# A two-layer attention and MLP decode step: a ring of three places instead of four, and one more quarter of a key cache kept between the layers

## The chip, the cores and the metric

The kernel runs on one core of a Trainium2 chip. The metric is the device time of one execution in microseconds; lower is better. The engines are named as in the profile: PE multiplies matrices, DVE and POOL work on vectors, ACT evaluates activations and copies, SP issues the DMAs. SBUF is the on-chip memory of 128 partitions, PSUM the small memory that PE writes to.

## The reference

Two tokens (one for each of B = 2 batch rows) pass twice through the same attention block and the same gated MLP. All data are float32.

```python
# x (2, 1, 576); k_cache, v_cache (2, 32, 8192, 128); wq (576, 4096); wo (4096, 576)
# w_gate, w_up (576, 4608); w_down (4608, 576)
def A(x):                                       # attention, H = 32 heads, Dh = 128
    q = heads(x @ wq)
    p = softmax(q @ k_cache^T * Dh ** -0.5)
    return merge(p @ v_cache) @ wo
def B(x):                                       # GEGLU
    return (gelu(x @ w_gate) * (x @ w_up)) @ w_down
x = x + A(layernorm(x)); x = x + B(layernorm(x))   # layer 0
x = x + A(layernorm(x)); x = x + B(layernorm(x))   # layer 1, same caches, same weights
```

The two caches hold 268 MB each and do not fit in SBUF, so both layers read them from memory.

## The kernel before, in words

**Items.** A layer's attention is cut into 34 items. Items 0 to 29 are pairs of heads of one batch row, with 8 MB of keys and 8 MB of values each. Items 30 to 33 (`SINGLE`) are one head each, with keys and values in four quarters of 1024 KB (`PART`, 2048 numbers in each partition). K31 below means the keys of item 31, V33 the values of item 33. Layer 0 walks the items from 0 to 33, layer 1 from 33 to 0. What layer 0 used last can therefore stay for layer 1: K32 and K33 (`KEYS_HELD`), V31, V32 and V33 (`VALUES_HELD`), and one quarter of K31.

**The memory.** Loads go into one SBUF tile, `space`: five slots of four `PART`s, and behind them, at `RING`, a ring of `NPLACE` places of 1152 KB (`PLACE`). The slots hold keys and values. The ring carries what lies between the two walks: the eight groups of layer 0's `wo`, the first MLP's gate, up and down weights, layer 1's `wq`, and the first quarters of keys of layer 1. `arena` remembers who owns what.

**The order of the loads.** `plan_first`, `plan_mlp(0)`, `plan_second` and `plan_mlp(1)` write one list by hand. `pump()` issues its loads in that order on SP's queue (L165 caches, L296 and L298 `wo`, L238 and L227 `wq`, L248 and L258 gate and up, L271 and L275 down) as soon as their place has been handed over, and each `done(key)` frees a place and calls `pump()` again. SP is in order: a load that waits for its place to be read holds back every load behind it.

**Scores.** For a part of keys, `multiply` forms keys times query (L644 on DVE) and folds the two halves of the head dimension (L661 on POOL); `add_up` reduces them (L664 on DVE) and frees the part. For the first five items of layer 1 (33 to 29) the work is spread: of 16 rows in each partition DVE multiplies 12 and POOL 4 (L648), ACT sums 7 (L654) and DVE reduces 9; POOL's share uses a copy of the query (`qs`, L643 on ACT), made at an item's first part. Softmax, values (L762 on PE) and the division follow; `project` (L812) multiplies by `wo`. In layer 0 the products of K32 and K33 must not overwrite the keys, so they go into two buffers, which `products()` takes from places of the ring.

**The kept quarter.** In layer 0 ACT copies K31's quarter 3 to the PSUM tile `kept` (L636) before it is overwritten. In layer 1 quarters 0 to 2 of K31 are loaded again; when quarter 0 is summed, ACT copies `kept` into its place (L679), which then serves as quarter 3.

The MLP's matmuls are at L951 (gate and up) and L1004 (down), the normalization's transposes and means at L494 to L535, the query's matmul at L549. All line numbers are those of the kernel before.

Of the kernel before, what the change touches and what calls it, by code (L numbers as in the profile page):

```python
# [36 lines left out]
PART = JC * DH  # L37
SLOT = 4 * PART
NSLOT = 6
PLACE = DF // 2  # L40
NPLACE = 4
RING = 5 * SLOT
END = RING + NPLACE * PLACE
HELD = 5


# [17 lines left out]
SINGLE = range(PAIRS, N)  # L64
# [3 lines left out]
class Arena:  # L68
# [32 lines left out]
    def ring(self, key, n):  # L101

        at = self.take(key, RING + self.turn % NPLACE * PLACE, n)
        self.turn += at is not None
        return at

    def fit(self, key, n, lo=0):

        for at in [self.at, lo] + sorted(end for _, end in self.live.values()):
            if lo <= at and at + n <= END and self.take(key, at, n) is not None:  # L110
                self.at = at + n
# [11 lines left out]
def decode_layers(ctx, tc, x_in, kc, vc, wq, wo, wg, wu, wd, out):  # L123
    nc = tc.nc
# [7 lines left out]

    space = consts.tile([P, END], F32, name="space")

# [10 lines left out]
    arena = Arena()  # L145
    queue, ready, places = [], {}, {}

    def pump():
        while queue and queue[0]():
            queue.pop(0)  # L150

    def done(key):
        arena.free(key)
        pump()

    def part_at(at, n):
        return space[:, at:at + n]

    def part(at):
        return part_at(at, PART).rearrange("p (j d) -> p j d", d=DH)  # L160

    def load(at, n, src, lo, hi):

        t = part_at(at, (hi - lo) * PART).rearrange("p (j d) -> p j d", d=DH)
        nc.sync.dma_start(t, ITEMS[n].source(src)[:, lo * JC:hi * JC, :])  # L165

    def cache(key, src, n, slots=None, pieces=None):
# [14 lines left out]

        queue.append(make)

    def half(key, src, n, k, slot):

        def make():
            at = arena.slots(key, (slot,), 4, k)
            if at is None:
                return False  # L190
            load(at[0], n, src, k, k + 4)
            ready.setdefault(key, {}).update((k + i, part(a)) for i, a in enumerate(at))
            return True

        queue.append(make)
# [83 lines left out]
    def products():  # L279

        def make():
            at = [RING + k * PLACE for k in (2, 3)]
            if not all(arena.clear(a, PLACE) for a in at):
                return False
            ready["products"] = [part(arena.take(("products", k), at[k], PART)) for k in range(2)]
            return True

        queue.append(make)
# [28 lines left out]
    def groups(layer):  # L317
        return range(H // GH)[::1 - 2 * layer]

    def name(kind, layer, n):  # L320

        return kind, 1 if n in (KEYS_HELD if kind == "k" else VALUES_HELD) else layer, n

    def plan_first():
        def k(n, *at):
            cache(name("k", 0, n), kc, n, *at)

        def v(n, *at):
            cache(name("v", 0, n), vc, n, *at)

        for us in three:
            half_rows(("wq", 0, us[0]), wq, us, END - NU * H * DH // 2)
        last = PAIRS - 1
        k(0)
        for n in range(1, PAIRS):
            k(n)
            v(n - 1)
        k(SINGLE[0], (0,))
        half(("v", 0, last), vc, last, 0, 1)
        half(("v", 0, last), vc, last, 4, 5)  # L340
        k(SINGLE[1], (3,))
        v(SINGLE[0], (4,))

        k(SINGLE[2], (2,))
        products()
        k(SINGLE[3], (0,))
        v(SINGLE[1], (4,))
        v(SINGLE[2], (3,))
        for g in groups(0)[:2]:
            out_rows(0, g)  # L350

        v63 = ("v", 1, SINGLE[3])
        places[v63] = [SLOT + k * PART for k in range(4)]
        for k in range(4):
            if k == 2:
                for g in groups(0)[2:4]:
                    out_rows(0, g)
            one(v63, vc, SINGLE[3], k, (v63, k))
        for g in groups(0)[4:]:
            out_rows(0, g)  # L360

    def plan_second():

        for k in range(4):
            of_half(1, k)
        half_rows(("wq", 1, NU - 1), wq, single[-1], None)
        for k in range(4):
            of_half(0, k)
        last = PAIRS - 1
        k63, v63, k62, v62 = ("k", 1, SINGLE[3]), ("v", 1, SINGLE[3]), ("k", 1, SINGLE[2]), ("v", 1, SINGLE[2])  # L370

        for k in range(3):
            one(("k", 1, SINGLE[1]), kc, SINGLE[1], k, None)
        for k in range(4):
            one(("k", 1, SINGLE[0]), kc, SINGLE[0], k, (k63, k - 1) if k else None)

        one(("k", 1, last), kc, last, 0, (k63, 3))
        turns = iter(range(1, 5)), iter(range(4))
        for kind in "vvvvkkkk":
            if kind == "k":  # L380
                k = next(turns[0])
                one(("k", 1, last), kc, last, k, (k62, k - 1))
            else:
                k = next(turns[1])
                one(("v", 1, SINGLE[0]), vc, SINGLE[0], k, (v63, k))
        for k in range(5, 8):
            one(("k", 1, last), kc, last, k, (v62, k - 5))
        half(("k", 1, last - 1), kc, last - 1, 0, 5)
        half(("k", 1, last - 1), kc, last - 1, 4, 4)
        half(("v", 1, last), vc, last, 0, 0)  # L390
        half(("v", 1, last), vc, last, 4, 1)
        for n in range(last - 2, -1, -1):
            cache(("k", 1, n), kc, n)
            cache(("v", 1, n + 1), vc, n + 1)
        cache(("v", 1, 0), vc, 0, None, (4, 2, 1, 1))
        for g in groups(1):
            out_rows(1, g)
# [80 lines left out]
    kept = psum1.tile([P, JC, DH], F32, name="kept")  # L478
# [62 lines left out]
    def attention(layer):  # L541
# [30 lines left out]
        else:  # L572
            half_products(1)
            key = ("wq", 1, NU - 1)
# [55 lines left out]
        def multiply(n, k, m):  # L630

            if k == 0:
                S[n] = work.tile([P, SK * 2 // P], F32, name="S")
            u = t = keys(n, k, m)
            if n == SINGLE[1] and k == 3 and layer == 0:
                nc.scalar.copy(kept, t)  # L636
            if layer == 0 and n in KEYS_HELD:
                u = ready["products"][k % 2]
            every = m * JC
            rows = 12 if waited(n) else every  # L640
            q = qs[:, n % 2, :]
            if rows < JC and k == 0:
                nc.scalar.copy(q, qb[n])  # L643
            nc.vector.tensor_tensor(  # L644
                out=u[:, :rows, :], in0=t[:, :rows, :], in1=qb[n].unsqueeze(1).to_broadcast([P, rows, DH]), op=ALU.mult
            )
            if rows < JC:
                nc.gpsimd.tensor_tensor(  # L648
                    out=u[:, rows:, :], in0=t[:, rows:, :], in1=q.unsqueeze(1).to_broadcast([P, JC - rows, DH]),
                    op=ALU.mult,  # L650
                )
            r = own_rows(n, k, m)
            for j in range(r, every):
                nc.scalar.activation(  # L654
                    u[:, j, :], u[:, j, :], AF.Copy, accum_out=S[n][:, k * JC + j:k * JC + j + 1]
                )
            if at_once(n, k):
                prod[n, k] = u[:, :r, :]
                return
            half = prod[n, k] = u[:, :r, :DH // 2]  # L660
            nc.gpsimd.tensor_tensor(out=half, in0=half, in1=u[:, :r, DH // 2:], op=ALU.add)  # L661

        def add_up(n, k, m):
            nc.vector.tensor_reduce(  # L664
                out=S[n][:, k * JC:k * JC + own_rows(n, k, m)], in_=prod.pop((n, k)), axis=AX.X, op=ALU.add
            )
            if layer == 0 and n in KEYS_HELD:
                if n == N - 1 and k >= 2:
                    done(("products", k - 2))
                return  # L670
            key = name("k", layer, n)
            for k in range(k, k + m - 1):
                done((key, k))
            k += m > 1
            if layer == 1 and n == SINGLE[1]:

                if k == 0:
                    ready[key][3] = ready[key][0]
                    nc.scalar.copy(ready[key][3], kept)  # L679
                    return  # L680
                k = k % 3
            done((key, k))
            if k == ITEMS[n].parts - 1 or not any(c == key for c, _ in arena.live):
                ready.pop(key)
# [148 lines left out]
        for i, n in enumerate(seq):  # L833
            last = i == N - 1
            p = seq[i - 1] if i else None

            v = {N - 2: None, N - 1: N - 3}.get(i, i - 1) if layer == 0 else i - 1
            a = seq[i - 2] if i > 1 and completes(i - 2) and not (layer == 0 and last) else None
# [53 lines left out]
        n, p = seq[-1], seq[-2]  # L892
# [154 lines left out]
```

## Time and profile before

| | |
|---|---|
| median of 3 runs | 2686.73 us (2686.35 to 2687.53) |
| span of the profiled execution | 2685.0 us |
| bytes read | 1153.18 MB |
| busy: PE, DVE, ACT, POOL | 34%, 67%, 6%, 43% |
| loads' queue, share of 16 DMA engines | 99.8% |
| mean rate | 430 GB/s |

The span runs from the first to the last instruction of the profiled execution, which is 1.7 us shorter than the median. Times in the views are microseconds from the start of that span. Layer 0's attention ends at about 1290 us, its MLP at 1369, and layer 1's keys begin to load at 1384. In the timelines a row is: start, duration, engine, line, operation, output, inputs, count, and in brackets the idle time before with what ended it. In the table of windows a row is: window, then busy time and instruction count for PE, weight loads, DVE, ACT and POOL, the granted clock of PE, the DMA share and GB/s.

### The profile page before, as it was taken

What the parts mean: (1) busy time and instruction counts of PE and PEld (TensorE: products, weight loads), DVE (VectorE), ACT (ScalarE), POOL (GpSimd) and SP (SyncE); (2) the same over time, 40 slices, a digit from 0 to 9 for tenths busy, and PEclk for the clock granted to TensorE, in tenths of its full rate; (3) what the DMA queues carried; (4) which work ended last, traced back from release to release, by engine and by line L of the source; (5) the groups of instructions that cost most, each with busy time, mean ns of one, the idle gap of its engine ahead of it and who ended that gap; (6) DMA issues with size and microseconds to landing.
All of it is one profiled execution on the core that took longest, in us unless ns stands there. A gap on an engine that the chain in (4) does not pass through costs nothing. (4 is left out here: it accounts for less than half of the span.)

```text
span 2685.0 us, 17174 instructions
## 1 busy us (share of the span) xinstructions
PE 914.4 (34%) x7150; PEld 305.4 (11%) x7150; DVE 1806.0 (67%) x874; ACT 163.7 (6%) x786; POOL 1161.8 (43%) x261
## 2 busy tenths in 40 slices
PE   1323332332233233334663333233223323332356
PEld 0100010010001000111221101001000100010022
DVE  4876687677667766867037877667766776776640
ACT  0000000000000000000026000000000000000000
POOL 2543454354445444544028455445444543454420
PEclk7656666665666566566986665666566656656678
DMA  9999999999999999999999999999999999999998
GB/s 422 436 436 426 437 432 434 433 434 432 433 431 435 436 428 433 436 428 425 414 418 434 431 431 436 431 434 434 437 428 434 434 435 431 431 434 435 433 421 375
DMA packets 33950, 1154.30 MB, mean 430 GB/s; under 512 B 4152, under 2 KB 4176, under 8 KB 5968
## 3 DMA queue, kind: packets, MB, share of 16 engines
q1 hardware_dynamic: 33832, 1153.19, 99.8%
q8 instruction: 56, 0.92, 0.1%
q14 instruction: 22, 0.18, 0.0%
q10 hardware_dynamic: 40, 0.01, 0.0%
HBM read 1153.18 MB, written 0.00 MB: 429 GB/s over the span
## 5 line engine op out<-in xcount | busy, mean ns | idle before, releaser
L661 POOL TENSOR_TENSOR space<-space 128x3072 f32<-128x3072 f32 (+3 forms) x221 | 1128.6, 5107 | 1263.3 <-DVE space L644 1202.5
L644 DVE TENSOR_TENSOR space<-space,bank 128x6144 f32<-128x6144 f32 (+3 forms) x223 | 1112.7, 4991 | 560.2 <-DMA space<-in_A_k_cache_dram 496.8
L762 PE MATMUL acc<-space,prz 128*8 128x512 f32 x4096 | 594.6, 744 | 199.4 <-DMA space<-in_A_v_cache_dram 195.5
L664 DVE TENSOR_REDUCE S<-space 128x48 f32<-128x3072 f32 (+3 forms) x223 | 569.3, 2553 | 89.9 <-POOL space L661 89.6
L592 PE MATMUL bank<-qsb,pick 4*64 4x128 f32 (+1 forms) x256 | 46.3, 436 | 863.1 <-DVE space L644 853.1
L762 PEld LDWEIGHTS acc<-space,prz 128*8 128x8 f32 x4096 | 119.1, 104 | 616.3 <-issue 410.6
L784 PE MATMUL bank<-of,osb 128*32 128x2 f32 x512 | 40.9, 202 | 324.4 <-DVE osb L777 324.4
L713 ACT ACTIVATE nbs<-bank 128x2 f32<-128x2 f32 (+1 forms) x68 | 11.6, 171 | 1848.2 <-PE bank L698 1801.8
L592 PEld LDWEIGHTS bank<-qsb,pick 4*64 4x64 f32 (+1 forms) x256 | 20.7, 202 | 882.5 <-DVE space L644 863.2
L517 POOL TENSOR_TENSOR rstd<-ve,mhalf 128x1 f32<-128x1 f32 x4 | 2.2, 550 | 168.8 <-DVE ve L515 168.8
L690 PE MATMUL bank<-ident,m 128*1 128x128 f32 x68 | 19.5, 286 | 160.7 <-DVE m L688 160.5
L784 PEld LDWEIGHTS bank<-of,osb 128*32 128x32 f32 x512 | 35.9, 154 | 331.7 <-DVE osb L777 330.5
L978 DVE STREAM_TRANSPOSE o<-o 128x288 f32<-128x288 f32 x4 | 2.8, 691 | 94.5 <-ACT o L976 94.5
L729 PE MATMUL bank<-sums,unit 128*128 128x2 f32 x120 | 35.2, 363 | 87.0 <-ACT prz L721 87.0
L776 DVE TENSOR_TENSOR acc<-acc,diag 128x512 f32<-128x512 f32 x64 | 43.5, 680 | 22.0 <-PE acc L762 22.0
L721 ACT ACTIVATE prz<-S,nbs 64x128 f32<-64x128 f32 (+1 forms) x128 | 50.7, 396 | 17.3 <-POOL prz L711 14.4
L803 ACT ACTIVATE oT<-bank,rinv 32x8 f32<-32x8 f32 x110 | 28.5, 259 | 381.5 <-PE bank L784 380.8
L654 ACT ACTIVATE space<-space 128x128 f32<-128x128 f32 x164 | 48.3, 296 | 23.6 <-DVE space L644 21.7
L698 PE MATMUL bank<-m,unit 1*128 1x2 f32 (+1 forms) x136 | 39.0, 354 | 25.3 <-DVE m L696 25.3
L777 DVE TENSOR_REDUCE osb<-acc 128x128 f32<-128x512 f32 x64 | 44.3, 691 | 2.2
L521 DVE TENSOR_TENSOR x<-bank,x 128x144 f32<-128x144 f32 x4 | 1.2, 308 | 64.1 <-PE bank L1004 40.4
L729 PEld LDWEIGHTS bank<-sums,unit 128*128 128x128 f32 x120 | 30.1, 311 | 92.2 <-ACT prz L721 92.2
(73 smaller groups left out, 427.6 us busy)
## 6 DMA issues: line engine op xcount, KB each, us to landing
space<-in_A_v_cache_dram SPq DMA_DIRECT2D x8, 4096.0 KB
space<-in_A_k_cache_dram SPq DMA_DIRECT2D x6, 4096.0 KB
space<-in_A_wo_dram SPq DMA_DIRECT2D x15, 1152.0 KB
space<-in_A_k_cache_dram SPq DMA_DIRECT2D x15, 1024.0 KB
space<-in_B_w_down_dram SPq DMA_DIRECT2D x9, 1152.0 KB
space<-in_B_w_gate_dram SPq DMA_DIRECT2D x3, 3456.0 KB
space<-in_A_v_cache_dram SPq DMA_DIRECT2D x10, 1024.0 KB
space<-in_A_wq_dram SPq DMA_DIRECT2D x3, 3072.0 KB
```

Of the source, the lines that this page charges most:

```text
L592: nc.tensor.matmul(qb[n][to, :], pick[32 * c:32 * c + 4, r:r + 1].to_broadcast([4, P // it.heads]), qsb[32 * c:32 * c + 4, (h % 4) * DH:(h ...
L644: nc.vector.tensor_tensor(out=u[:, :rows, :], in0=t[:, :rows, :], in1=qb[n].unsqueeze(1).to_broadcast([P, rows, DH]), op=ALU.mult)
L654: nc.scalar.activation(u[:, j, :], u[:, j, :], AF.Copy, accum_out=S[n][:, k * JC + j:k * JC + j + 1])
L661: nc.gpsimd.tensor_tensor(out=half, in0=half, in1=u[:, :r, DH // 2:], op=ALU.add)
L664: nc.vector.tensor_reduce(out=S[n][:, k * JC:k * JC + own_rows(n, k, m)], in_=prod.pop((n, k)), axis=AX.X, op=ALU.add)
L698: nc.tensor.matmul(mT[n][:, :heads], ones[0:1, :], m1[:, :heads], start=True, stop=True)
L721: nc.scalar.activation(pr[at, lo:].rearrange("p (g e) -> p g e", e=4)[:, 0:it.rows // 2:2, :], s[at, :it.rows].rearrange("p (g r) -> p g r ...
L729: nc.tensor.matmul(tot[n][:, :ITEMS[n].heads], ones, rs.pop(n), start=True, stop=True)
L762: nc.tensor.matmul(accumulator(n)[32 * c:32 * c + 8, :], pr[:, at:at + 8], t[g // 4][:, g % 4 * 4:g % 4 * 4 + 4, :].rearrange("p j d -> p ...
L776: nc.vector.tensor_tensor(out=q, in0=q, in1=diag.unsqueeze(2).to_broadcast([P, 4, DH]), op=ALU.mult)
L777: nc.vector.tensor_reduce(out=t, in_=q.rearrange("p r d -> p d r"), axis=AX.X, op=ALU.add)
L784: nc.tensor.matmul(po[lo:lo + 32, i, :], t[:, i::GH], of, start=True, stop=True)
```

## The change

The ring has three places. The fourth place becomes `KEPT`, in which K31's quarter 3 is loaded in layer 0 and stays for layer 1; `SCRATCH`, the last part of slot 3, takes its products in layer 0. The PSUM tile `kept` now holds quarter 2 of K31: ACT copies it out in layer 0 one quarter earlier, and in layer 1 back into the place of quarter 0, where it serves as quarter 2. Layer 1 loads only quarters 0 and 1 of K31. The two buffers of `products()` move to places 1 and 2. In layer 0 the second half of V29 and the whole of K31 are each loaded as three parts and one part instead of four.

```diff
 PLACE = DF // 2
-NPLACE = 4
+NPLACE = 3
 RING = 5 * SLOT
-END = RING + NPLACE * PLACE
+KEPT = RING + NPLACE * PLACE
+END = KEPT + PART
+SCRATCH = 3 * SLOT + 3 * PART
...
+    def some(key, src, n, k, at):
+        def make():
+            if not all(arena.clear(a, PART) for a in at):
+                return False
+            for i, a in enumerate(at):
+                arena.take((key, k + i), a, PART)
+            load(at[0], n, src, k, k + len(at))
+            ready.setdefault(key, {}).update((k + i, part(a)) for i, a in enumerate(at))
+            return True
+        queue.append(make)
...
-            at = [RING + k * PLACE for k in (2, 3)]
+            at = [RING + k * PLACE for k in (1, 2)]          # products()
...
         half(("v", 0, last), vc, last, 0, 1)
-        half(("v", 0, last), vc, last, 4, 5)
-        k(SINGLE[1], (3,))
+        some(("v", 0, last), vc, last, 4, [5 * SLOT + k * PART for k in range(3)])
+        some(("v", 0, last), vc, last, 7, [SCRATCH])
+        k61 = name("k", 0, SINGLE[1])
+        some(k61, kc, SINGLE[1], 0, [3 * SLOT + k * PART for k in range(3)])
+        some(k61, kc, SINGLE[1], 3, [KEPT])
...
-        for k in range(3):
+        for k in range(2):
             one(("k", 1, SINGLE[1]), kc, SINGLE[1], k, None)
...
-            if n == SINGLE[1] and k == 3 and layer == 0:     # multiply()
-                nc.scalar.copy(kept, t)
+            if n == SINGLE[1] and layer == 0:
+                if k == 2:
+                    nc.scalar.copy(kept, t)
+                elif k == 3:
+                    u = part(arena.take(("scratch", 0), SCRATCH, PART))
...
+            if layer == 0 and n == SINGLE[1] and k == 3:     # add_up()
+                ready.pop(key)
+                ready["k", 1, n] = {3: part(KEPT)}
+                done(("scratch", 0))
+                return
...
                 if k == 0:
-                    ready[key][3] = ready[key][0]
-                    nc.scalar.copy(ready[key][3], kept)
-                    return
-                k = k % 3
+                    ready[key][2] = ready[key][0]
+                    nc.scalar.copy(ready[key][2], kept)
+                else:
+                    done({1: (key, 1), 2: (key, 0), 3: (("k", 0, n), 3)}[k])
+                if k == 3:
+                    ready.pop(key)
+                return
             done((key, k))
```

## The prediction

> **What bounds the kernel now.** I read the page first: busy time by engine, then the slices, then the DMA queues.
>
> ```profile
> span 2685.0 us, 17174 instructions
> PE 914.4 (34%) x7150; PEld 305.4 (11%) x7150; DVE 1806.0 (67%) x874; ACT 163.7 (6%) x786; POOL 1161.8 (43%) x261
> DMA  9999999999999999999999999999999999999998
> q1 hardware_dynamic: 33832, 1153.19, 99.8%
> HBM read 1153.18 MB, written 0.00 MB: 429 GB/s over the span
> ```
>
> No compute engine is above 67%, while the one load queue keeps the 16 DMA engines occupied for 99.8% of the span and no slice of 67 us falls below nine tenths except the last. So the time is bytes over rate, plus whatever time the queue runs dry. The profiled span is 2685.0 us; the three runs have a median of 2686.73 us, 1.7 us more. I work out differences against the profiled execution and add them to the median.
>
> Because the DMA is never visibly idle, the whole question is where the change could make it idle. That depends on how early each load is issued before the load ahead of it has landed. I read that lead from three views: the timeline of SP (when a load is issued), the waits of PE (a matmul that begins when a weight lands dates that landing), and the DMA view of one window for the rate there.
>
> **The load that goes.** The change removes one load of a quarter of K31, 1024 KB or 1.0486 MB. Rate at that place, from the DMA view of 1390 to 1437 us:
>
> ```profile
> DMA packets 2663, 20.02 MB, mean 426 GB/s; under 512 B 298, under 2 KB 298, under 8 KB 298
> space<-in_A_k_cache_dram SPq DMA_DIRECT2D x12, 1024.0 KB
> space<-in_A_v_cache_dram SPq DMA_DIRECT2D x4, 1024.0 KB
> ```
>
> 1.0486 MB / 426 GB/s = 2.46 us. That is the ceiling of the gain: 0.09% of the span. Two other loads of 4096 KB (V29's second half, K31 in layer 0) become 3072 + 1024 KB each, the same bytes in two more instructions. The Trainium skill, DMA: Bandwidth & Descriptors, section "Anatomy of one DMA", gives a fixed cost of about 2.0 us for each DMA beside its bytes; charged to every queued load it would take 4.0 us for the two splits and give back 2.0 with the removed one, so that the whole sum below would be 3.2 us and the time 2689.9 us. The rows above speak against charging it to a queued load: loads nearly all of 1024 KB run at 426 GB/s, so consecutive ones cost about their bytes and I take 0 for the splits.
>
> **What an idle queue costs to restart.** The only place in the trace where the queue starts from nothing is the beginning:
>
> ```profile
> 0.74 6.96 SPq L227 DMA_DIRECT2D space<-in_A_wq_dram  x3
> 0.00:1.00 1.00, 0.00 (x0) 0.00 (x0) 0.17 (x3) 0.00 (x0) 0.41 (x5) 1.00 0.00 0
> 1.00:2.00 1.00, 0.00 (x0) 0.00 (x0) 0.62 (x7) 0.00 (x0) 0.29 (x1) 1.00 0.95 246
> 2.00:3.00 1.00, 0.00 (x0) 0.00 (x0) 0.91 (x7) 0.00 (x0) 0.00 (x0) 1.00 0.42 147
> 3.00:4.00 1.00, 0.00 (x0) 0.00 (x0) 0.89 (x4) 0.00 (x0) 0.00 (x0) 1.00 0.92 393
> 4.00:5.00 1.00, 0.00 (x0) 0.00 (x0) 0.78 (x3) 0.00 (x0) 0.00 (x0) 1.00 1.04 444
> 2682.00 0.64 SPq L1019 DMA_DIRECT2D out_dram<-x  x1
> ```
>
> The last column is GB/s. By 5.00 us 246 + 147 + 393 + 444 = 1230 KB have come, worth 2.9 us at 430 GB/s; the data effectively began at 2.1 us, 1.4 us behind the issue at 0.74. The other end: the small store issued at 2682.00 has to be complete before the span ends at 2685.0, 3.0 us from issue to completion. So a load that is issued into an empty queue effectively starts 1.4 to 3.0 us after its issue. I take 2.7, near the upper end, because what releases work is the completion of the last of 16 engines, as in the store's row.
>
> **The ring with three places.** Here a place is loaded as soon as the matmuls of the load before it in that place are done.
>
> ```profile
> 1299.48 1.16 PE L951 MATMUL acc<-space,xt 128*8 128x288 f32 x16 [0.35 <-DMA space<-in_B_w_gate_dram]
> 1302.25 1.16 PE L951 MATMUL acc<-space,xt 128*8 128x288 f32 x16 [1.20 <-DMA space<-in_B_w_gate_dram]
> ```
>
> A place takes 2.77 us to land, and PE needs 1.16 us for it, after which SP issues. With four places three loads are queued behind a landing; with three, two: 2 x 2.77 - 1.2 = 4.3 us of lead, against a restart of 1.4 to 3.0. So the steady ring costs nothing; the cover left is 1.3 us. Three starts of the ring are tighter.
>
> ```profile
> 1233.48 0.86 SPq L296 DMA_DIRECT2D space<-in_A_wo_dram  x2
> 1234.39 0.90 SPq L165 DMA_DIRECT2D space<-in_A_v_cache_dram  x2
> SPq L296 <- DVE S L664: 23.1, 1, 23.1
> 1258.46 2.95 SPq L296 DMA_DIRECT2D space<-in_A_wo_dram  x2
> 1272.04 1.17 PE L812 MATMUL bank<-space,oT 128*4 128x144 f32 x32 [1.30 <-DMA space<-in_A_wo_dram]
> 1296.75 1.11 SPq L258 DMA_DIRECT2D space<-in_B_w_gate_dram  x2
> 1372.97 0.33 SPq L227 DMA_DIRECT2D space<-in_A_wq_dram  x1
> 1375.51 1.04 PE L549 MATMUL acc<-space,xt 128*4 128x512 f32 x8 [1.03 <-DMA space<-in_A_wq_dram]
> ```
>
> First, wo. The two product buffers of K32 and K33 move to places 1 and 2, so the second group of wo, which is now issued at 1233.9, waits with the third for DVE's last sums (1258.46, the wait of 23.1 us). Behind it on SP stand the first two quarters of V33. What lands at 1272.04 is the third wo group; taking off its 1152 KB (2.8 us), two quarters of V33 (4.9) and the second group (2.8), the first group lands at about 1261.5, 3.1 us after the new issue at 1258.46. That just covers the restart, with nothing to spare, so I take 0.2 us, 0 to 0.5. Second, the first MLP: its fourth gate piece now waits for the first piece's matmuls, which in this trace release the issue at 1296.75, and the third piece lands at 1299.48: lead 2.7 us, cost 0 to 0.3, taken 0.1. Third, layer 1's query weights: the fourth piece of the first half waits for the first piece's matmuls, behind the normalization (issue at 1372.97), and the third lands at 1375.51: lead 2.5 us, cost 0 to 0.5, taken 0.2. Sum 0.5 us (0 to 1.3). With these the order of the bytes is unchanged.
>
> **The copy from PSUM.** This is the part that decides, by my reading. In layer 1 item 31's four quarters are multiplied in order on DVE. The quarter in PSUM comes back by a copy on ACT (L679). Before it is the last quarter; after, the third. The timelines of ACT and DVE:
>
> ```profile
> 1421.45 1.84 ACT L679 COPY space<-kept 128x2048 f32<-128x2048 f32 x1
> 1427.00 0.30 ACT L654 ACTIVATE space<-space 128x128 f32<-128x128 f32 x1
> 1427.29 0.25 ACT L643 COPY qs<-bank 128x128 f32<-128x128 f32 x1
> 1419.60 1.73 DVE L644 TENSOR_TENSOR space<-space,bank 128x1536 f32<-128x1536 f32 x1
> 1423.32 1.75 DVE L644 TENSOR_TENSOR space<-space,bank 128x1536 f32<-128x1536 f32 x1 [0.28 <-ACT space L679]
> 1424.99 0.75 DVE L664 TENSOR_REDUCE S<-space 128x9 f32<-128x576 f32 x1
> 1427.58 1.75 DVE L644 TENSOR_TENSOR space<-space,bank 128x1536 f32<-128x1536 f32 x1 [1.83 <-ACT qs L643]
> ```
>
> The copy stands on ACT's in-order queue behind the second quarter's sums and a softmax, so it does not end sooner. DVE multiplies the third quarter at 1419.60 while the copy is still to come, and only the fourth waits for it, at 1423.32. After, the third waits until 1423.32. Then the fourth follows the third's 1.75 us and one reduction of 0.75, at about 1425.8, ending at 1427.5; ACT's seven sums of it, 0.30 us each, end at 1429.6; the query copy of item 30 (L643, 0.25), queued behind them, ends at 1429.85, and item 30's first multiply starts at 1429.9 instead of 1427.58: 2.3 us later. The quarter already in SBUF cannot help, as its multiply stands behind the third's on DVE.
>
> Who waits for it: the load of K28's first half, into the places of K31 and K30's first quarter. SP issues it when item 30's first quarter is summed.
>
> ```profile
> 1432.83 0.33 SPq L165 DMA_DIRECT2D space<-in_A_k_cache_dram  x1
> 1442.17 0.33 SPq L165 DMA_DIRECT2D space<-in_A_k_cache_dram  x1
> 1390.38 1.04 PE L549 MATMUL acc<-space,xt 128*4 128x512 f32 x8 [1.04 <-DMA space<-in_A_wq_dram]
> 1466.84 0.33 SPq L165 DMA_DIRECT2D space<-in_A_k_cache_dram  x1
> ```
>
> The last query weights land at 1390.38. Behind them come 19 loads of 1024 KB (15 of K, 4 of V), 19 x 2.46 = 46.7 us, so the queue is empty at 1437.1: K28's issue at 1432.83 has 4.3 us of lead, and no time is lost. After, 18 loads are left and the queue is empty at 1434.6, but the issue comes at 1432.83 + 2.3 = 1435.1, and data flow at 1435.1 + 2.7 = 1437.8 (1436.5 to 1438.1 over the restart's range). Against 1437.1 before: +0.7 us (-0.6 to +1.0). The 2.46 us are not lost to another transfer; they become 3.2 us of an empty queue.
>
> K28's second half (1442.17 + 2.3 = 1444.5) is issued 3.1 us before the first half's 4.19 MB end at 1437.8 + 9.8 = 1447.6, just covered. K27 (1466.84 + 2.3) has V29's 8.39 MB ahead of it, which end after 1437.8 + 39.4 = 1477, and keeps 8 us. From there all loads move as a block to the end.
>
> The ACT copy in layer 0 also moves one quarter ahead. DVE waits there 3.96 us for the load of K32, more than the copy's 1.84 us, so I take nothing:
>
> ```profile
> 1229.61 2.29 DVE L644 TENSOR_TENSOR space<-space,bank 128x2048 f32<-128x2048 f32 x1 [3.96 <-issue]
> ```
>
> The sum: +0.7 at K28, +0.5 at the ring's starts, +1.2 us. On the median that is 2687.9 us. Its own bounds: -0.6 + 0 to +1.0 + 1.3, that is 2686.1 to 2689.0.
>
> **The rivals.** (1) The plain gain. If the copy's move doesn't delay item 30, K28 is issued at 1432.83 with 1.8 us of lead before 1434.6, against a restart of 1.4 to 3.0: 0 to 1.2 us lost, 1.3 to 2.5 us gained, 2684.2 to 2685.4. For it: ACT is idle for long in the span (6% busy), and a scheduler might place the copy ahead. Against it: in the built program the copy has the same place in ACT's queue. (2) Slower: the ring. If a load in mid-stream needs more than 4.3 us from issue to landing beyond its own transfer, each of the 44 loads of the ring (8 of wo, 27 of the MLP, 9 of the query weights) loses the rest: at 4.6 us, 0.3 x 44 = 13 us, 2700 us; 0.13 us each is enough to be slower. For it: in the ring DMA moves less than elsewhere already,
>
> ```profile
> 1300.00:1310.00 10.00, 5.76 (x68) 1.83 (x60) 0.00 (x0) 0.00 (x0) 0.00 (x0) 1.00 1.00 398
> ```
>
> 398 GB/s. Against it: the busy share in the same row is 1.00, so the low rate is not a wait. (3) That no load goes away: the built program issues one load of a quarter less in layer 1, so I give it nothing.
>
> **The numbers.** One measurement of this kernel can tell about 0.2% from no change, 5.4 us, so faster means below 2681.4 and slower above 2692.1. The likeliest case (spent at K28) gets 0.65, the plain gain 0.20, the ring 0.13, and 0.02 is left for a gain beyond the removed bytes, for which I see no mechanism. All of the first two cases is within 0.2%: faster 0.02, same 0.85, slower 0.13. The range takes in the plain gain's end, 2684.2, and reaches upward from 2689.0 to the edge of the ring's case, 2692.0; left out are the ring and the unexplained gain, 0.15.
>
> **What would show it.** Right: in the timeline of SP after, K28's first half is issued about 2.3 us later than before, the copy is followed by the third quarter's multiply, and the DMA's rate falls in the window of 1434 to 1438; the waits keep SP's long wait for DVE at wo. Wrong: K28's issue no later than before (then the plain gain), or shares of DMA below 1.0 all through 1262 to 1390 us (then the ring). A change of more than 2.5 us downward would refute the bytes' price, and one of more than 2.4 us upward the restart's.

## The result, and the profile after

The changed kernel takes 2695.8 us (median of 5 runs, 2693.33 to 2699.6), the kernel before 2686.73 us (2686.35 to 2687.53): slower by a factor of 1.0035, 95% interval 1.0023 to 1.0048. I had forecast 2687.9 us and a range up to 2692.0. The profiled execution of the changed kernel spans 2694.0 us, 9.0 more than before, so its trace shows the whole loss. The five runs also spread over 6.3 us where five of before spread over 1.2.

The page of the changed kernel, busy time, slices and the load queue:

```profile
span 2694.0 us, 17166 instructions
PE 917.7 (34%) x7150; PEld 305.2 (11%) x7150; DVE 1805.8 (67%) x874; ACT 164.0 (6%) x786; POOL 1161.9 (43%) x261
DMA  9999999999999999999999999999999999999998
GB/s 421 435 435 434 430 431 434 430 435 432 433 432 434 435 434 431 429 429 414 395 391 416 438 429 435 431 434 434 433 433 434 431 433 435 429 433 433 433 423 376
```

The DMA's busy digits are the same as before, 9 in every slice but the last. Only the line below them has changed: 414, 395, 391 and 416 GB/s in slices 19 to 22, that is 1212 to 1482 us. Before, it read 425, 414, 418 and 434 at that place:

```profile
GB/s 422 436 436 426 437 432 434 433 434 432 433 431 435 436 428 433 436 428 425 414 418 434 431 431 436 431 434 434 437 428 434 434 435 431 431 434 435 433 421 375
```

The loss lies between the two walks, where the ring is.

The same stretch as one window, before and after (the last three columns are PE's granted clock, DMA busy share, GB/s):

```profile
1260.00:1400.00 140.00, 87.56 (x1105) 34.98 (x1095) 24.89 (x52) 10.76 (x59) 8.83 (x8) 0.94 1.01 416
```

```profile
1260.00:1400.00 140.00, 91.69 (x1105) 34.62 (x1097) 17.10 (x46) 5.23 (x22) 4.17 (x6) 0.91 1.00 394
```

The rate falls by 5.3%, from 416 to 394 GB/s, while the busy share only falls from 1.01 to 1.00 (by the DMA records from 1.006 to 0.991, which is 2.1 us of the 140). At the old rate the same bytes would have come 140 x (1 - 394/416) = 7.4 us earlier. DVE's busy time, 24.89 and 17.10 us, says the same: layer 1's scores begin later.

Where in the ring it accrues is read from matmuls that begin when a load lands. Before, then after: the third wo group, the last up piece of the first MLP, its last down piece (only after, where the row before was at 1367.25 us), and the last query weights.

```profile
1272.04 1.17 PE L812 MATMUL bank<-space,oT 128*4 128x144 f32 x32 [1.30 <-DMA space<-in_A_wo_dram]
1342.70 1.16 PE L951 MATMUL acc<-space,xt 128*8 128x288 f32 x16 [1.23 <-DMA space<-in_B_w_up_dram]
1367.25 1.16 PE L1004 MATMUL bank<-space,hT 128*4 128x144 f32 x32 [0.62 <-DMA space<-in_B_w_down_dram]
1390.38 1.04 PE L549 MATMUL acc<-space,xt 128*4 128x512 f32 x8 [1.04 <-DMA space<-in_A_wq_dram]
```

```profile
1273.04 1.16 PE L841 MATMUL bank<-space,oT 128*4 128x144 f32 x32 [2.15 <-DMA space<-in_A_wo_dram]
1346.11 1.16 PE L980 MATMUL acc<-space,xt 128*8 128x288 f32 x16 [1.42 <-DMA space<-in_B_w_up_dram]
1372.36 1.16 PE L1033 MATMUL bank<-space,hT 128*4 128x144 f32 x32 [0.67 <-DMA space<-in_B_w_down_dram]
1398.45 1.04 PE L567 MATMUL acc<-space,xt 128*4 128x512 f32 x8 [0.96 <-DMA space<-in_A_wq_dram]
```

The delay is 1.0 us at wo, 3.4 at the end of gate and up, 5.1 after down, 8.1 after the query weights (by the DMA records 0.6 us of it is there before the ring, at the first wo group). It grows along the whole ring, not at one place.

The part that I had called decisive is there too. DVE, ACT and SP of the changed kernel at item 31 and at K28's first and second half:

```profile
1429.53 1.84 ACT L705 COPY space<-kept 128x2048 f32<-128x2048 f32 x1
1431.40 1.75 DVE L665 TENSOR_TENSOR space<-space,bank 128x1536 f32<-128x1536 f32 x1 [3.65 <-ACT space L705]
1433.80 1.75 DVE L665 TENSOR_TENSOR space<-space,bank 128x1536 f32<-128x1536 f32 x1
1437.92 1.75 DVE L665 TENSOR_TENSOR space<-space,bank 128x1536 f32<-128x1536 f32 x1 [1.70 <-ACT qs L664]
1443.16 0.33 SPq L167 DMA_DIRECT2D space<-in_A_k_cache_dram  x1
1452.30 0.33 SPq L167 DMA_DIRECT2D space<-in_A_k_cache_dram  x1
```

The third quarter waits for the copy, 3.65 us. From that multiply to item 30's first are 6.5 us (forecast 1429.9 - 1423.3 = 6.6), and K28's issue follows 5.2 us behind that (forecast 5.2).

### The profile page after: what moved, and what is told of

It reads as the page before. It is cut to its first block, busy times and chain, and to the rows that moved or that the text cites. A ratio compares the mean times of both kernels' runs of the same rounds, so it can differ in the third digit from the quotient of the medians.

```text
span 2694.0 us, 17166 instructions
## 1 busy us (share of the span) xinstructions
PE 917.7 (34%) x7150; PEld 305.2 (11%) x7150; DVE 1805.8 (67%) x874; ACT 164.0 (6%) x786; POOL 1161.9 (43%) x261
## 5 line engine op out<-in xcount | busy, mean ns | idle before, releaser
L742 ACT ACTIVATE nbs<-bank 128x2 f32<-128x2 f32 (+1 forms) x68 | 11.6, 171 | 1847.1 <-PE bank L727 1800.7
```

## The experiments

**The ring alone, the order alone, the products alone, and two places.** Four kernels, measured on one chip together with the kernel before.

```diff
 # ring3_only: the kernel before with
-NPLACE = 4
-END = RING + NPLACE * PLACE
+NPLACE = 3
+END = RING + 4 * PLACE
-            at = [RING + k * PLACE for k in (2, 3)]
+            at = [RING + k * PLACE for k in (1, 2)]
 # and item 30's first quarter at RING + 3 * PLACE
```

> The kernel before with a ring of three places and the product buffers in places 1 and 2; the fourth place is left empty, except that it takes item 30's first quarter of keys in layer 1. All three quarters of K31 are loaded again and the last comes from PSUM, as before: no load is removed and the copy is not moved. Theory R (the ring loses the time: in the changed kernel the loads' landings fall 7.9 us behind those of before between the first wo group and the first quarter of K31): about 2694 us, 6 to 10 us above before, with a wider spread of runs than before. Theory C (the copy's move at the start of layer 1 and the product buffers at wo make most of the loss): 2687 to 2689 us.

Measured: 2695.71 us (2693.97 to 2699.32), ratio 1.0033 (1.0021 to 1.0046). Three places (with the products' move that they need), with every load still there and the copy in its old position, cost 9.0 us: as much as the whole change, with a similar spread of runs, 5.4 us. Its window:

```profile
1260.00:1400.00 140.00, 87.62 (x1105) 34.45 (x1097) 17.24 (x46) 5.23 (x22) 3.61 (x4) 0.95 0.99 393
```

```diff
 # copy_last: the changed kernel with, in units(),
+            if layer == 1 and n == SINGLE[1]:
+                return [(k, 1) for k in (0, 1, 3, 2)]
 # and K31 is handed over after quarter 2
```

> The changed kernel, but in layer 1 item 31's quarters are multiplied in the order 0, 1, 3, 2, so that the quarter copied back from PSUM is the last again. Theory R: the ring's 8 us stay; K28's first half is issued about 2.3 us earlier relative to item 31's start, and 1 to 2.3 us are won against the changed kernel: 2693.5 to 2695 us. Theory C: 2687 us or less. If the copy's place costs nothing: 2695.8 us as the changed kernel.

Measured: 2695.38 us (2692.12 to 2696.32), ratio 1.0030 (1.0019 to 1.0041). The ring's loss stays. Against the changed kernel the median is 0.4 us lower, less than the spread of either, so this pair doesn't size the copy; copy_third below measures it in the kernel before.

```diff
 # products12: the kernel before with
-            at = [RING + k * PLACE for k in (2, 3)]
+            at = [RING + k * PLACE for k in (1, 2)]
```

> The kernel before with four places, and one edit: the product buffers lie in places 1 and 2 instead of 2 and 3, so that the second wo group and two quarters of V33 wait for DVE's last sums as in the changed kernel. My prediction gave this step 0.2 us (0 to 0.5): 2686.9 us. If the lead that the DMA engines lose there is paid back later in the ring: 2688 to 2690 us.

Measured: 2687.58 us (2687.18 to 2689.86), ratio 1.0004 (0.9995 to 1.0013). The medians are 0.9 us apart and the interval holds 1, so the step is small; the interval's upper end, 3.5 us, still leaves most of the 9 us to the place count.

```diff
 # ring2_only: the kernel before with NPLACE = 2; products, K31's third
 # and item 30's first quarter in the two places beside the ring
```

> The kernel before with a ring of two places; products, K31's third and item 30's first quarter have places of their own beside the ring, so nothing else waits longer. With two places one load of 2.77 us is queued behind a landing, less 1.2 us of matmuls: 1.6 us of lead. A restart of 2.7 us, as predicted, makes each of some 44 loads lose 1.1 / 2 to 1.1 us: 25 to 50 us. A restart of 4 to 5 us on the slowest engine (theory R's reading of why three places lose) makes it 2.4 to 3.4 us each or half of that: 55 to 150 us.

Measured: 2729.63 us (2724.14 to 2730.37), ratio 1.0160 (1.0145 to 1.0176): 43 us, 1.0 us for each of 44 loads. That lies in the range of my restart, not in that of the longer one.

**Halved places.** In the same memory, twice as many loads of half the size. They were meant to lengthen the lead.

```diff
 # half_places: copy_last with
+HALF_PLACE = PLACE // 2
-        at = self.take(key, RING + self.turn % NPLACE * PLACE, n)
-        self.turn += at is not None
+        at = self.take(key, RING + self.turn % (2 * NPLACE) * HALF_PLACE, n)
+        self.turn += (1 if n <= HALF_PLACE else 2) if at is not None else 0
 # and each ring load and its matmuls in two halves; half_before: the same in the kernel before
```

> The changed kernel with item 31's quarters multiplied in the order 0, 1, 3, 2, and with the ring cut into six places of 576 KB in the same memory: every weight load of the ring is halved, and each half is freed after its own matmuls. If a ring of three places loses because 4.3 us queued behind a landing is too little for the slowest engine's restart (2.5 to 5.4 us from issue to data in the two-place run), the lead of 5 x 1.39 - 0.7 = 6.2 us brings nearly all of the ring's 8 to 9 us back: 2685.5 to 2688 us. If it loses because of the number of separate loads or places that are handed over, twice as many make it worse: 2700 us or more.

> The kernel before with its four places cut into eight of 576 KB in the same way: what halving the loads costs by itself, where the lead was already enough (7.1 us, now 9 us). 2686.5 to 2688 us if rows of half the length move at the same rate; 2690 us or more if shorter rows or more issues on SP cost a few per cent of the 125 us in which the ring is read.

Measured: half_places 2698.36 us (2697.39 to 2699.09), ratio 1.0043 (1.0030 to 1.0055); half_before 2692.35 us (2691.47 to 2693.98), ratio 1.0021 (1.0012 to 1.0030). Halving costs 5.7 us in the kernel with four places. The window from 1310 to 1345 us, of half_before and then of before, shows a full busy share at a lower rate:

```profile
1310.00:1345.00 35.00, 21.75 (x221) 5.47 (x214) 1.87 (x7) 0.97 (x3) 0.00 (x0) 0.95 1.02 408
```

```profile
1310.00:1345.00 35.00, 20.50 (x216) 6.79 (x216) 2.34 (x8) 1.47 (x4) 0.00 (x0) 0.95 1.01 422
```

But the lead did not become longer. SP's waits in the same window (total us, times, longest) are, in half_before and then in before:

```profile
SPq L254 <- DMA space<-in_B_w_up_dram: 3.5, 15, 0.8
SPq L254 <- DMA space<-in_B_w_gate_dram: 2.8, 14, 0.2
SPq L267 <- PE acc L989: 0.2, 1, 0.2
```

```profile
SPq L248 <- PE acc L951: 7.0, 5, 1.6
SPq L248 <- DMA space<-in_B_w_gate_dram: 4.0, 5, 1.0
```

Before, SP waits mostly for the matmuls that free a place. In half_before it waits for earlier loads to land. These programs count the landings of their loads on eight semaphores, and no trace of this case has more than eight loads issued and not landed; from 1290 to 1345 us 62 of half_before's 73 issues come within 0.1 us of the landing of the load eight before. A piece of gate or up is two loads, so eight loads are four whole pieces or four halves. From an issue to the landing of the load ahead of it the median in this stretch is 7.6 us before, 5.0 in half_before and half_places, and 5.1 in ring3_only (counted for every load; the 4.3 us of the prediction are worked out for a piece). The halving shortened the lead to that of three places, and the lead of 6.2 us that was expected for half_places was not there.

So the pair doesn't test a longer lead. What it shows fits the ring: with four places too, a lead of 5.0 us comes with a loss. How much of the 5.7 us is the shorter lead and how much the shorter rows (4608 bytes at 25.9 GB/s on one DMA engine in the median, where before moves rows of 9216 at 26.5) was not separated.

**The restart, the copy and the removed load, each by itself.**

```diff
 # ring1_only: the kernel before with NPLACE = 1, the other quarters in places beside it
```

> The kernel before with a ring of one place (products, K31's quarters 1 and 2 and item 30's first quarter have places beside it), so that each of the 42 to 44 weight loads starts into an empty queue. It measures the restart by itself: the time from SP's issue to the first matmul, less the load's own 2.5 to 2.8 us. With my 2.7 us (1.4 to 3.0): 44 x (2.7 + 1.2) = 172 us above before (115 to 185). Theory R needs restarts of the slowest engine that reach over 4.3 us now and then: single loads of 7 us and more from issue to matmul, and a mean above 3 us: 185 to 230 us above before.

Measured: 2885.81 us (2 runs), ratio 1.0739 (1.0720 to 1.0759): 199 us, 4.5 us for each of 44 loads. PE's rows in the down projection:

```profile
1460.52 2.10 PE L1005 MATMUL bank<-space,hT 128*4 128x144 f32 x32 [3.76 <-DMA space<-in_B_w_down_dram]
1468.02 2.10 PE L1005 MATMUL bank<-space,hT 128*4 128x144 f32 x32 [3.72 <-DMA space<-in_B_w_down_dram]
1475.53 1.99 PE L1005 MATMUL bank<-space,hT 128*4 128x144 f32 x32 [3.72 <-DMA space<-in_B_w_down_dram]
```

A load's cycle is 7.5 us: 2.1 of matmuls (PE's granted clock is 0.60 in this kernel's window of 1260 to 1400 us, shown further down), 2.7 of transfer (1152 KB at 433 GB/s), and 2.7 for the restart. My 2.7 was right, and the restart from an empty queue is fairly steady: the seven cycles from 1460.52 to 1513.39 us lie between 7.46 and 7.66. The 199 us lie above my 172, as the matmuls took 2.1 us and not 1.2. Theory R, as I had put it, needed restarts that now and then reach 4.3 us. An empty queue doesn't show them: by the DMA records a load issued in one DMA with nothing ahead of it takes 2.2 to 3.3 us beyond its transfer.

```diff
 # copy_third: the kernel before with
-            if n == SINGLE[1] and k == 3 and layer == 0:
+            if n == SINGLE[1] and k == 2 and layer == 0:
-        for k in range(3):
+        for k in (0, 1, 3):
             one(("k", 1, SINGLE[1]), kc, SINGLE[1], k, None)
 # and kept copied back as quarter 2
```

> The kernel before with its four places, and one edit: the PSUM tile holds K31's quarter 2 instead of 3, and layer 1 loads quarters 0, 1 and 3. No load is removed. By my chain K28's first half is issued 2.3 us later, at 1435.1, with 2.0 us of lead before the queue empties at 1437.1: 0.7 us are lost with a restart of 2.7 us, up to 2.3 us with one of 4.3: 2687.4 to 2689.0 us. If the copy's place doesn't matter: 2686.7 us.

Measured: 2688.9 us (2687.97 to 2689.9, 11 runs), ratio 1.0007 (0.9998 to 1.0016). All runs lie above the median of before, 2.2 us between the medians, though the interval still just holds 1. SP issues K28's first half at

```profile
1435.17 0.33 SPq L165 DMA_DIRECT2D space<-in_A_k_cache_dram  x1
```

against 1432.83 before: 2.3 us, as forecast. The queue runs dry ahead of it. The rate from 1434 to 1452 us, in 40 slices of 0.45 us, with the busy digits above it; the fall to 164 and 0 GB/s lies between 1434.5 and 1437.6 us:

```profile
DMA  9653999059099198591991981919927970971957
GB/s 401 273 237 164 583 492 473 0 218 947 0 583 583 73 728 364 218 874 73 510 655 73 728 364 73 1019 73 291 510 73 218 655 291 0 874 291 73 874 218 291
DMA packets 310, 6.95 MB, mean 386 GB/s; under 512 B 38, under 2 KB 38, under 8 KB 38
```

Before, the same stretch moved 7.75 MB:

```profile
DMA packets 333, 7.75 MB, mean 431 GB/s; under 512 B 38, under 2 KB 38, under 8 KB 38
```

The 0.8 MB that are missing are 1.9 us at 426 GB/s. By the DMA records the first engine has ended the last quarter before K28 at 1434.9 us, ahead of the issue, and the last engine ends it only at 1437.5. The first engine ends K28's first half 1.9 us later than before and the last one 0.2; at the second half, which is issued at 1445.24 (before 1442.17), the last one too is 2.4 us later.

```diff
 # one_less: the kernel before with, in one(),
+            if (key, k) != (("k", 1, SINGLE[1]), 2):
                 load(at, n, src, k, k + 1)
```

> The kernel before with its four places, without the load of K31's quarter 2 in layer 1 (the scores are then computed from what lies in that place); nothing else is changed. What the removed 1024 KB are worth alone: 2.46 us, less what is lost where the queue now has one load less of lead (V30's first quarter, K28's first half): by my working 1.3 to 2.5 us, 2684.2 to 2685.4 us; if all of it is lost at these two loads, 2686.7 us.

Measured: 2687.13 us (2686.4 to 2688.93, 11 runs), ratio 1.0001 (0.9992 to 1.0011). The removed megabyte, with four places and the copy in its old position, wins nothing by the medians (the interval's lower end is a gain of 2.1 us). The DMA view of 1400 to 1412 us shows where it goes, of one_less and then of before:

```profile
DMA  9988996999999999999999999799989999345979
GB/s 382 300 273 300 382 437 273 410 410 437 410 437 437 437 410 437 437 437 410 437 437 437 410 382 382 328 355 382 382 355 410 328 328 273 137 191 246 355 300 382
DMA packets 601, 4.41 MB, mean 367 GB/s; under 512 B 63, under 2 KB 63, under 8 KB 63
```

```profile
DMA  9999999999999999999999999999999999999999
DMA packets 694, 5.09 MB, mean 424 GB/s; under 512 B 73, under 2 KB 73, under 8 KB 73
```

0.68 MB of the 1.05 MB saved are not moved in these 12 us. SP's rows say why. Item 30's third quarter and V30's first are issued at the same time in both, because they wait for item 33's sums and values and not for the queue:

```profile
1396.09 5.08 SPq L165 DMA_DIRECT2D space<-in_A_k_cache_dram  x3
1405.14 4.70 SPq L165 DMA_DIRECT2D space<-in_A_v_cache_dram  x4
```

```profile
1396.03 5.06 SPq L165 DMA_DIRECT2D space<-in_A_k_cache_dram  x3
1405.07 3.50 SPq L165 DMA_DIRECT2D space<-in_A_v_cache_dram  x4
```

**PE or DMA.** In the changed kernel's ring some pieces take PE 2.11 us where the others take 1.16:

```profile
1318.86 1.16 PE L980 MATMUL acc<-space,xt 128*8 128x288 f32 x16 [2.00 <-DMA space<-in_B_w_up_dram]
1321.65 2.11 PE L980 MATMUL acc<-space,xt 128*8 128x288 f32 x16 [1.63 <-DMA space<-in_B_w_gate_dram]
1324.42 2.11 PE L980 MATMUL acc<-space,xt 128*8 128x288 f32 x16
1331.46 1.16 PE L980 MATMUL acc<-space,xt 128*8 128x288 f32 x16 [2.70 <-DMA space<-in_B_w_gate_dram]
```

A load is late (2.00 us of waiting), PE takes 0.95 us longer for the next two pieces, their places are handed over that much later, and the load at 1331.46 is later still. The Trainium skill, TensorE: Matmul & The Clock Gate, "Part 1: The HAM clock gate", has the array at half speed after an idle window of about 3.4 us. The trace agrees in the clock, 0.50 from 1320.4 to 1327.2 us, where a piece takes 2.11 us against 1.16; the single waits are shorter here, 2.00 and 1.63 us with matmuls between them. Two kernels fill more of PE's gaps:

```diff
 # ring3_warm: ring3_only, and last_warm: copy_last, with
-                    idle_products(1)
+                    idle_products(2)
-    IDLE = [(2, 2, 2, 2, 2, 2, 2, 2, 1), ...
+    IDLE = [(2, 3, 3, 3, 3, 3, 3, 3, 2), ...
```

> The three-place ring alone (the kernel before with an empty fourth place), with twice the idle matmuls between the weight pieces (three instead of two in the down projection), so that PE waits less and none of its pieces takes 1.7 to 2.1 us instead of 1.16. In the changed kernel's trace several lost steps follow such a slow piece (a piece of 2.11 us at 1321.65, then an issue at 1323.81 and a load that is 1.5 us late). If slow pieces, which shorten the lead from 4.3 to 3.3 us, cause the loss: 3 to 6 us won against 2695.7, that is 2690 to 2693 us. If the loss comes from the DMA's side (first rows of a load that an engine reaches soon after its issue): 2694 to 2697 us.

> The changed kernel with item 31's order 0, 1, 3, 2 and twice the idle matmuls in the ring: the best form of the change that the runs so far point to. With the loss on PE's side 2689 to 2692 us; on the DMA's side 2694 to 2696 us. Below 2686.7 us only if the ring's whole loss went away.

Measured: ring3_warm 2694.75 us (2692.6 to 2696.76), ratio 1.0029 (1.0019 to 1.0039); last_warm 2694.35 us (2692.14 to 2696.79), ratio 1.0029 (1.0019 to 1.0039). Both are 1.0 us below the kernels that they were made from, which is within the spread. The window of ring3_warm:

```profile
1260.00:1400.00 140.00, 100.78 (x1175) 40.21 (x1167) 18.99 (x47) 5.38 (x23) 4.27 (x7) 0.98 1.00 400
```

PE's clock rises from 0.95 to 0.98 and the rate from 393 to 400 GB/s, where before has 416. Both times are those expected if the loss comes from the DMA's side. The traces say the same of the slow pieces: from 1285 to 1400 us the changed kernel has 8 that take over 1.5 us, ring3_only 3, ring3_warm and last_warm one each, and the kernel before 2. Three places lose 9.0 us with three slow pieces and 8.1 with one, so PE's clock is at most a small part of it. The greater part is on the DMA's side. No version of the change came below the kernel before.

## Why the prediction was wrong, point by point

**What bounds the kernel** was right: the DMA, and the question where the change lets it run dry.

**The step that failed is the ring.** I took a lead of 4.3 us behind a landing against a restart of 1.4 to 3.0 us and concluded that "the steady ring costs nothing; the cover left is 1.3 us", with 0.5 us (0 to 1.3) for its three starts. ring3_only measured 9.0 us. The lead was worked out correctly and so was the restart (2.7 us in ring1_only), but the comparison of the two doesn't decide. It treats the queue as one server that is either empty or not, and counts the lead to the landing, which is the end of the last of 16 engines. What the traces show instead is a gradual loss: with one place the rate of the window is 183 GB/s, with two 326, with three 393, with four 416.

Ring1_only's window, then ring2_only's:

```profile
1260.00:1400.00 140.00, 61.77 (x543) 19.87 (x539) 9.20 (x27) 1.58 (x6) 0.83 (x3) 0.60 0.51 183
```

```profile
1260.00:1400.00 140.00, 82.03 (x1017) 32.87 (x1009) 13.66 (x43) 2.55 (x9) 1.24 (x3) 0.88 0.89 326
```

The sixteen DMA engines don't finish a load together. In the trace of the kernel before, the first and the last of them end the second wo group 4.8 us apart (DMA records), and a late engine is no loss as long as it isn't the last. In the changed kernel they end it 1.3 us apart: the group's issue at 1259.1 us comes after the first engine has ended the load ahead (1257.3), so the early engines had run out. From the issue of a load to the first engine's end of the load ahead, the median from 1262 to 1390 us is 3.2 to 3.3 us in the five kernels with three places, 3.6 to 5.2 in the four with four whole places, and 3.3 to 3.4 in the two halved ones: with three places not far above the restart of 2.7. Long rows also become more frequent. From 1310 to 1345 us, 37 packets of the changed kernel took over 0.4 us more than their bytes at 27 GB/s (a sixteenth of 430); before it was 1; from 1375 to 1400 us 43 and 4. These long packets count as busy: over the window of 140 us they hold 3.7 us more of each engine than before, beside the 2.1 us by which the share falls, of 7.4 us lost. That they come where an engine reaches a load soon after its issue fits ring1_only, where most engines have one at each restart, but it was not tested by itself. Why three places lose 9 us when the steady restart leaves 1.3 us of cover therefore stays partly open: the place count is shown to be the cause, and PE's clock to be at most a small part of it; that early engines run out and then have long packets is read from the records and argued, as no run changed it by itself.

**The rival of the ring was dismissed by a wrong reading.** I had named it, priced it at 13 us, and given it 0.13, with this against it: "the busy share in the same row is 1.00, so the low rate is not a wait". The changed kernel's window has a share of 1.00 and lost 7.4 us. The share counts the long packets as busy; the rate shows the bytes that are missing. My sign for this rival, "shares of DMA below 1.0 all through 1262 to 1390 us", is met only in part: the share is 0.99 from 1310 to 1345 us, 1.00 to 1370 and 0.98 to 1390. Its mechanism, a load that needs more than 4.3 us, was not shown either.

**The copy** was right in mechanism and in its delay (2.3 us at K28's issue in copy_third, 6.5 and 5.2 us along the chain in the changed kernel), and too small in price. I had the second half of K28 "just covered"; it lost as well. copy_third costs 2.2 us. By my sum the delay should have cost 0.7 + 2.46 = 3.2 us after one load less, but with the load still there 2.0 us of lead against 2.7, that is 0.7.

**The removed load** was priced at 2.46 us for its bytes. one_less, which only removes it, is 0.4 us above before (interval 0.9992 to 1.0011). My sum had let the lost lead show at K28 alone; K30's third quarter and V30's first, which wait for item 33, come earlier and lose it first. I read SP's issues around K28 and not those from 1396 to 1405 us. So the plain gain, to which I gave 0.20, was by the medians not there even without the copy's move.

**The products** at wo: 0.2 us forecast, 0.9 measured, with an interval that holds 0.

The parts as measured: +9.0 for three places (which includes the products), +2.2 for the copy and +0.4 for the load, 11.6 in sum, against +9.1 for the change. Parts measured in the kernel before need not add up in the changed one; copy_last is only 0.4 us below it, and what the copy costs there stays open.

## What to carry to other kernels

When a stream is limited by DMA, don't judge a ring's depth by whether its lead exceeds the restart from an empty queue; here a lead of 4.3 us against 2.7 still lost 9 us, and only a run with one place less showed it. Read the rate (GB/s) beside the busy share: a share of 1.00 hides losses of 5%. And a megabyte removed from a queue is only worth its time if no load behind it waits for compute before the queue would have run out.

## What the runs showed of the hardware that I had not expected

A restart from an empty queue is fairly steady, 2.5 to 2.8 us in the eight loads of ring1_only's down projection. The Trainium skill, DMA: Bandwidth & Descriptors, "Anatomy of one DMA — SWDGE (gpsimd) path", gives about 2.0 us of fixed cost, fitted for DMAs issued from GpSimd, a condition that the prediction left out; the loads here are issued from SP and show about 0.7 more. A queue that is nearly empty loses more than that lets one think: 4.5 us a load with one place, 1.0 with two, 0.2 with three. The changed kernel's runs spread over 6.3 us and those of ring3_only over 5.4, against 1.2 before: with a thin lead the time itself is less certain. Halving the pieces to 576 KB cost 5.7 us: with at most eight loads in flight, loads of half the size also halve the bytes that are queued.
